# Late modulation vectors: from TensorE row products to VectorE dot products over transposed weights

## Chip, cores, metric

One core of a Trainium2 chip. The metric is device time in microseconds, the median of several executions. Engines: PE is TensorE, DVE is VectorE, ACT is ScalarE, POOL is GpSimd, SP is SyncE, which issues nearly all DMA here.

## The reference, cut to what matters

```python
mod = (silu(c) @ w_mod).reshape(1, 6, 1, -1)      # c: [1,1024], w_mod: [1024, 6*1024], bf16
sa, ca, ga, sb, cb, gb = mod[:, 0] ... mod[:, 5]  # six vectors of 1024
h = layernorm(x) * (1 + ca) + sa                  # x: [2048, 1024]
x = x + ga * attention(h)                         # 32 heads of 128, 512 keys, 4 kv heads
h = layernorm(x) * (1 + cb) + sb
x = x + gb * swiglu(h)                            # hidden size 3584
```

The vectors `sa` and `ca` are needed in the first microseconds. The other four are the late ones: `ga` at the end of the first attention chunk, `cb` and `sb` at the second norm, `gb` in the feed-forward part.

## The kernel before

The attention part runs in 128 steps (4 chunks of 512 rows, 32 heads). In each step PE does scores, a query projection, an output-projection unit and the product with v, and DVE evicts PSUM (copies PE's results out of its accumulator memory). `at(k, f, ...)` hangs a task on step k. The late vectors are made as rows: `silu(c)` is spread over 32 columns, and four narrow matmuls (128x32 weights) run side by side.

```python
sil32 = const.tile([P, DT, 32], BF16, name="sil32")
for dt in range(DT):                              # eight DVE broadcasts, in the start-up
    nc.vector.tensor_scalar(out=sil32[:, dt, :], in0=ones_bf[:, 0:32],
                            scalar1=siluc[:, dt:dt + 1], scalar2=None, op0=ALU.mult)
# ...
def mod_rows(n, part):                            # four calls: steps 5, 13, 21, 29
    ps = mm("row_ps")
    tiles = [wm_rows.pop(0) for _ in range(2)]
    for k in range(4):
        for i in range(4):                        # four column tiles: 16 matmuls a burst
            nc.tensor.matmul(ps[32 * i:32 * i + 32, :], lhsT=sil32[:, 4 * part + k, :],
                             rhs=tiles[i // 2][:, k, (i % 2) * 512:(i % 2 + 1) * 512],
                             start=(k == 0), stop=(k == 3))
    # ... evict, add the two parts, store rows to DRAM ...
def load_cols(n, k, dst, add_one):                # steps 16 and 32
    src = row_d[n][k:k + 2, :].rearrange("a (b p) -> p (a b)", p=P)
    fetch(out=dst, in_=src)                       # 1024 values come back as columns
    if add_one:                                   # only at step 16
        nc.vector.tensor_scalar(out=dst, in0=dst, scalar1=1.0, scalar2=None, op0=ALU.add)
```

The weight-norm bound (sums of squares of the weights, on DVE) already uses the instruction that the change will use, and four of its products are clipped to the same step 32:

```python
def bound_wq(hg, i, j):
    # ...
    pin(nc.vector.scalar_tensor_tensor(out=junk, in0=w, scalar=1.0, in1=w, op0=ALU.mult,
                                       op1=ALU.mult, accum_out=sq[:, col:col + 1]))
# ...
at((1 + hg % (NTC - 1)) * H + max(0, 4 * hg - 3 + 2 * i + j), bound_wq, hg, i, j)
```

The weight-norm bound (sums of squares of the weights, on DVE) already uses the instruction that the change will use.

The second norm: normalised rows (`xn`), crossbar transposes (the DMA transposes a block on its way), affine operations (times a vector, plus a vector).

Of the kernel before, what the change touches and what calls it, by code (L numbers as in the profile page):

```python
# [9 lines left out]
ALU = mybir.AluOpType  # L10
AX = mybir.AxisListType
BF16 = mybir.dt.bfloat16
FP32 = mybir.dt.float32
# [575 lines left out]
def fast_path(ctx, tc, flag, A_x, A_k_cache, A_v_cache, A_wq, A_wo, B_x, B_w_gate, B_w_up,  # L589
# [3 lines left out]
    nc = tc.nc  # L593
    P = 128
    _, S, D = A_x.shape
    _, Hkv, Sk, Dh = A_k_cache.shape
# [6 lines left out]
    TCW = 512  # L603
    NTC = S // TCW
    QT = TCW // P
    DT = D // P
# [17 lines left out]
    wm_v = w_mod.rearrange("(dt p) n -> p dt n", p=P)  # L624
# [4 lines left out]
    const = ctx.enter_context(tc.tile_pool(name="const", bufs=1))  # L629
    xpool = ctx.enter_context(tc.tile_pool(name="xres", bufs=1))  # L630
    hpool = ctx.enter_context(tc.tile_pool(name="hT", bufs=4))
# [3 lines left out]
    wk = ctx.enter_context(tc.tile_pool(name="work", bufs=2))  # L635
    sm = ctx.enter_context(tc.tile_pool(name="small", bufs=4))
    psp = ctx.enter_context(tc.tile_pool(name="psum", bufs=4, space=bass.MemoryType.PSUM))
    dp = ctx.enter_context(tc.tile_pool(name="dram", bufs=4, space=bass.MemoryType.DRAM))
# [7 lines left out]
    def blkC(name, shape, dt=BF16):  # L646
        return pc_.tile(shape, dt, name=name, tag="C")

    def mm(name, shape=(P, 512), dt=FP32):
        return psp.tile(list(shape), dt, name=name, tag="mm", bufs=4)  # L650
# [9 lines left out]
    def pin(ins, what="steps"):  # L660
        return tc.keep_in_program_order(ins) if stage[what] else ins

    def fetch(out, in_):
        pin(nc.sync.dma_start(out=out, in_=in_), "dma")  # L664

    def load(out, in_):
        with nc.allow_non_contiguous_dma(reason="weight slice"):
            fetch(out=out, in_=in_)
# [33 lines left out]
    for kv in range(Hkv):  # L702
        pin(nc.sync.dma_start_transpose(
            out=kT[:, kv, :], in_=A_k_cache[0, kv, k0:k0 + W, :]), "dma")
# [10 lines left out]
    ones_bf = const.tile([P, P], BF16, name="ones_bf")  # L715
# [15 lines left out]
    sa, ca1, sb, cb1 = (modT[:, i, :] for i in range(4))  # L731
    ga_bc = const.tile([P, D], FP32, name="ga_bc")
    gb_bc = const.tile([P, D], FP32, name="gb_bc")
# [7 lines left out]
    sil_r = const.tile([DT, P], BF16, name="sil_r")  # L741
# [3 lines left out]
    siluc = const.tile([P, DT], BF16, name="siluc")  # L745
# [12 lines left out]



    sil32 = const.tile([P, DT, 32], BF16, name="sil32")
    for dt in range(DT):
        nc.vector.tensor_scalar(out=sil32[:, dt, :], in0=ones_bf[:, 0:32],
                                scalar1=siluc[:, dt:dt + 1], scalar2=None, op0=ALU.mult)
    wm_rows = []
    row_part = []
    row_d = {}

    def load_rows(vec, part):
        t = hpool.tile([P, 4, D], BF16, name="wmr", tag="hT")  # L770
        load(t, wm_v[:, 4 * part:4 * part + 4, vec * D:(vec + 1) * D])
        wm_rows.append(t)

    def mod_rows(n, part):
        ps = mm("row_ps")
        tiles = [wm_rows.pop(0) for _ in range(2)]
        for k in range(4):
            for i in range(4):
                nc.tensor.matmul(ps[32 * i:32 * i + 32, :], lhsT=sil32[:, 4 * part + k, :],  # L779
                                 rhs=tiles[i // 2][:, k, (i % 2) * 512:(i % 2 + 1) * 512],  # L780
                                 start=(k == 0), stop=(k == 3))
        if part == 0:
            r = blkC("row", [P, TCW], FP32)
            nc.vector.tensor_copy(out=r, in_=ps)
            row_part.append(r)
        else:
            r = row_part.pop()
            nc.vector.tensor_tensor(out=r, in0=ps, in1=r, op=ALU.add)
            d = dp.tile([4, TCW], FP32, name="row_d", tag="row_d", bufs=2)
            fetch(out=d, in_=r[0:P:32, :])  # L790
            row_d[n] = d

    def load_gate(n, k, dst):
        fetch(out=dst.rearrange("p (a b) -> p a b", a=2),
                          in_=row_d[n][k:k + 2, :].partition_broadcast(P))

    def load_cols(n, k, dst, add_one):
        src = row_d[n][k:k + 2, :].rearrange("a (b p) -> p (a b)", p=P)
        with nc.allow_non_contiguous_dma(reason="1024 values to columns"):
            fetch(out=dst, in_=src)  # L800
        if add_one:
            nc.vector.tensor_scalar(out=dst, in0=dst, scalar1=1.0, scalar2=None, op0=ALU.add)

    tasks = {}

    def at(k, f, *a):
        tasks.setdefault(k, []).append((f, a))


    hT = {}  # L810
# [15 lines left out]
    def ln_norm(tt, on_act=False):  # L826
        mv = ln.pop(tt)
        n = wk.tile([P, D], BF16, name="xn", tag="xn", bufs=3)
        if on_act:
            nc.vector.scalar_tensor_tensor(out=mv[:, 3:4], in0=mv[:, 0:1], scalar=-1.0,  # L830
                                           in1=mv[:, 2:3], op0=ALU.mult, op1=ALU.mult)
            nc.scalar.activation(out=n, in_=xt[tt], func=ACT.Identity, bias=mv[:, 3:4],
                                 scale=mv[:, 2:3])
        else:
            pin(nc.vector.tensor_scalar(out=n, in0=xt[tt], scalar1=mv[:, 0:1],
                                        scalar2=mv[:, 2:3], op0=ALU.subtract, op1=ALU.mult))
        return n
# [85 lines left out]
    for t in range(QT):  # L923
        ln_stats(t)
        n = ln_norm(t, t % 2 == 0)
# [5 lines left out]
    for half in range(DH):  # L931
# [6 lines left out]
        for n in range(4 * LEAD):  # L938
            dt, g = (4 * half + n // LEAD, n % LEAD) if half == 0 else (4 + n % 4, n // 4)
            nc.tensor.matmul(q0_ps[g],  # L940
                             lhsT=wq_tiles[(0, 0, dt // 4)][:, dt % 4, g * P:(g + 1) * P],
                             rhs=hT[("h1", 0)][:, dt, :], start=(dt == 0), stop=(dt == DT - 1))
# [168 lines left out]
            nc.vector.tensor_tensor(out=x1, in0=f, in1=x1, op=ALU.add)  # L1111


    for n, vecs in enumerate(((2, 4), (5, 3))):
        for part in range(2):
            k = 16 * n + 8 * part
            at(k, load_rows, vecs[0], part)
            at(k + 2, load_rows, vecs[1], part)
            at(k + 5, mod_rows, n, part)
        at(16 * n + 15, load_gate, n, 0, gb_bc if n else ga_bc)  # L1120
        at(16 * n + 16, load_cols, n, 2, sb if n else cb1, n == 0)
    for tt in range(QT, S // P):
        cc, t = divmod(tt, QT)
        at(max((cc - 1) * H - 16, 0) + 2 + 2 * t, load_x, tt)
# [116 lines left out]
def kernel(tc, *args):  # L1241
    nc = tc.nc
    with tc.tile_pool(name="guard", bufs=1) as gp:
        flag = gp.tile([1, 1], I32, name="flag")
        fast_path(tc, flag, *args)
        over = nc.values_load(flag[0:1, 0:1], min_val=0, max_val=1)
        with tc.If(over > 0):
            general_path(tc, *args)
# [30 lines left out]
```

## Time and profile before

| | before |
|---|---|
| time, median of 3 | 1283.59 us (1283.0 to 1285.08) |
| PE busy | 1270.0 us, 99% of the span |
| DVE busy | 577.3 us, 45% |

The page of the kernel before: busy time by engine, and the chain of waits by engine.

```profile
PE 1270.0 (99%) x7601; PEld 643.1 (50%) x7601; DVE 577.3 (45%) x1271; ACT 333.9 (26%) x433; POOL 1.2 (0%) x8
...
PE 96%; DMA 2%; DVE 1%; SPq 0%; ACT 0%; issue 0%; DVEq 0%
```

PE is the bound. Only its work, or a stop of it, moves the time. The groups of instructions of the kernel before (busy us, mean ns of one, idle before with its releaser):

```profile
L955 DVE SCALAR_TENSOR_TENSOR junk<-wq 128x1024 bf16<-128x1024 bf16 x32 | 38.9, 1215 | 0.0
...
L779 PE MATMUL row_ps<-wmr,sil 128*32 128x512 bf16 x64 | 4.2, 382 | 0.0
...
L802 DVE TENSOR_SCALAR modT<-modT 128x8 f32<-128x8 f32 x1 | 0.2, 172 | 3.6 <-DMA modT<-row_d 3.6
```

The 64 row matmuls of 382 ns are busy for 4.2 us only, since four run at once. The add-one (L802) kept DVE idle for 3.6 us. The waits of the kernel before (us in total, times, longest):

```profile
DVE modT L802 <- DMA modT<-row_d: 3.6, 1, 3.6
...
PE mod_ps L753 <- DMA wm<-in_w_mod_dram: 1.7, 1, 1.7
...
PE a_ps L1096 <- DVE acc L1102: 1.0, 1, 1.0
...
PE gu_ps L1173 <- DVE guT L1179: 0.8, 1, 0.8
```

A row burst in the timeline of the kernel before (start us, duration us, engine, line, operation):

```profile
44.73 1.89 PE L1019 MATMUL q_ps<-hT,wq 128*128 128x512 bf16 x8
...
46.55 1.05 PE L779 MATMUL row_ps<-wmr,sil 128*32 128x512 bf16 x16
...
47.52 0.29 PE L1064 MATMUL o_ps<-v_sb,pT 128*128 128x130 bf16 x2
```

From the first row matmul to the next work is 0.97 us. The stop behind the add-one, same view:

```profile
86.93 0.43 SPq L664 DMA_DIRECT2D modT<-row_d  x1
...
92.00 0.17 DVE L802 TENSOR_SCALAR modT<-modT 128x8 f32<-128x8 f32 x1 [3.62 <-DMA modT<-row_d]
...
92.69 0.67 DVE L1102 COPY acc<-a_ps 128x512 f32<-128x512 f32 x1
...
93.41 1.89 PE L1096 MATMUL a_ps<-wo,oT 128*128 128x512 bf16 x8 [0.99 <-DVE acc L1102]
```

The column read was issued at 86.93 us. DVE stood until 92.00, the eviction behind it came late, and PE stood 0.99 us for a free PSUM bank.

The busiest stretch of DVE, by windows of 10 us (busy us and instructions of PE, PEld, DVE, ACT, POOL; clock; DMA share; GB/s):

```profile
210.00:220.00 10.00, 10.00 (x72) 5.53 (x70) 8.46 (x19) 3.84 (x7) 0.00 (x0) 1.00 0.53 121
220.00:230.00 10.00, 10.00 (x72) 5.53 (x70) 8.74 (x21) 3.84 (x6) 0.00 (x0) 1.00 0.66 196
230.00:240.00 10.00, 10.00 (x72) 5.54 (x70) 8.53 (x18) 3.43 (x5) 0.00 (x0) 1.00 0.84 241
240.00:250.00 10.00, 10.00 (x72) 5.52 (x70) 8.81 (x19) 3.75 (x4) 0.00 (x0) 1.00 0.16 36
```

### The profile page before, as it was taken

How to read it: one execution, taken by the hardware profiler on the slowest of the kernel's cores; microseconds unless marked ns; L12 is line 12 of the kernel's file. 1: busy time of each engine (PE TensorE's matmuls, PEld its weight loads, DVE VectorE, ACT ScalarE, POOL GpSimd, SP SyncE). 2: the span in 40 equal slices, each digit the busy share in tenths (PEclk: the TensorE clock that was granted, in tenths of full speed). 3: DMA queues.
4: the chain of work that ended last, by engine and by line, in shares of the span. 5: the costliest groups of instructions: out<-in, count | busy, mean ns of one | idle time of the engine just before them, and what ended most of it. 6: DMA issues, size and time to landing. Idle time of an engine off the chain costs nothing.

```text
span 1283.0 us, 18137 instructions
## 1 busy us (share of the span) xinstructions
PE 1270.0 (99%) x7601; PEld 643.1 (50%) x7601; DVE 577.3 (45%) x1271; ACT 333.9 (26%) x433; POOL 1.2 (0%) x8
## 2 busy tenths in 40 slices
PE   8999999999999999999999999999999999999998
PEld 4555555555555555555554444444444444444444
DVE  4464557865577755576663642221212221221122
ACT  3543334343333433333341111011100111011100
POOL 0000000000000000000000000000000000000000
PEclk8999999999999999999999999999999999999999
DMA  9878566557355554445678484454536455454401
GB/s 286 275 187 234 169 149 171 133 142 204 98 124 156 148 140 148 116 149 131 132 195 247 129 249 149 139 189 147 180 103 218 140 164 164 135 193 134 129 22 47
DMA packets 280108, 204.21 MB, mean 159 GB/s; under 512 B 113865, under 2 KB 273609, under 8 KB 280018
## 3 DMA queue, kind: packets, MB, share of 16 engines
q1 hardware_dynamic: 275106, 198.78, 54.1%
q10 hardware_dynamic: 4912, 4.20, 1.0%
q8 instruction: 61, 1.00, 0.3%
q14 instruction: 29, 0.24, 0.1%
HBM read 174.08 MB, written 4.21 MB: 139 GB/s over the span
## 4 chain that ended last, share of the span: by engine, by line
PE 96%; DMA 2%; DVE 1%; SPq 0%; ACT 0%; issue 0%; DVEq 0%
PE gu_ps L1173 29%; PE a_ps L1096 17%; PE q_ps L1019 17%; PE d_ps L1193 15%; PE o_ps L1064 9%; PE s_ps L1032 8%; DMA wm<-in_w_mod_dram 1%; DMA hT<-xn 1%; PE q_ps L940 0%; DMA modT<-row_d 0%; PE row_ps L779 0%; SPq L664 0%; PE mod_ps L753 0%; DVE st L816 0%; ACT pT L1034 0%; PE h_ps L927 0%
## 5 line engine op out<-in xcount | busy, mean ns | idle before, releaser
L1034 ACT ACTIVATE pT<-s_ps 128x1024 bf16<-128x1024 f32 x256 | 248.7, 1020 | 341.8 <-PE s_ps L1032 341.8
L1096 PE MATMUL a_ps<-wo,oT 128*128 128x512 bf16 x1024 | 241.9, 379 | 1.0 <-DVE acc L1102 1.0
L1019 PE MATMUL q_ps<-hT,wq 128*128 128x512 bf16 x1000 | 236.7, 379 | 0.3 <-DVE modT L755 0.3
L1173 PE MATMUL gu_ps<-hT,wg 128*128 128x512 bf16 x896 | 211.7, 379 | 0.8 <-DVE guT L1179 0.8
L1179 DVE TENSOR_TENSOR guT<-gu_ps,sg 128x512 bf16<-128x512 f32 x112 | 77.4, 691 | 282.5 <-ACT sg L1178 282.5
L1178 ACT ACTIVATE sg<-gu_ps 128x512 bf16<-128x512 f32 x112 | 66.9, 597 | 489.6 <-PE gu_ps L1173 438.4
L1193 PE MATMUL d_ps<-wd,guT 128*128 128x512 bf16 (+2 forms) x952 | 194.2, 366 | 0.0
L916 DVE CAST qT<-q_ps 128x512 bf16<-128x512 f32 x128 | 88.2, 691 | 176.9 <-PE q_ps L1019 176.3
L1173 PE MATMUL gu_ps<-hT,wu 128*128 128x512 bf16 x672 | 163.3, 379 | 0.0
L1096 PEld LDWEIGHTS <-oT 128*128 128x128 bf16 x1024 | 99.9, 98 | 122.3 <-issue 2.1
L1019 PEld LDWEIGHTS <-wq 128*128 128x128 bf16 x1000 | 97.8, 98 | 117.8 <-issue 0.3
L1193 PEld LDWEIGHTS <-guT 128*128 128x128 bf16 x952 | 90.9, 98 | 103.0
L1064 PEld LDWEIGHTS <-pT 128*128 128x128 bf16 x2048 | 126.6, 98 | 30.6 <-issue 0.4
L1173 PEld LDWEIGHTS <-wg 128*128 128x128 bf16 x896 | 87.6, 98 | 106.5 <-issue 1.1
L1064 PE MATMUL o_ps<-v_sb,pT 128*128 128x130 bf16 x2048 | 137.1, 220 | 0.0
L1032 PE MATMUL s_ps<-qT,kT 128*128 128x512 bf16 x512 | 131.5, 379 | 0.6 <-ACT pT L1034 0.6
L1173 PEld LDWEIGHTS <-wu 128*128 128x128 bf16 x672 | 65.8, 98 | 79.3
L1051 DVE TENSOR_TENSOR oq<-o_ps,rl 128x256 bf16<-128x256 f32 (+2 forms) x256 | 101.2, 419 | 4.3
L1197 DVE TENSOR_TENSOR f<-d_ps,gb_bc 128x512 f32<-128x512 f32 (+2 forms) x34 | 22.4, 660 | 147.1 <-PE d_ps L1193 147.1
L1104 DVE TENSOR_TENSOR acc<-a_ps,acc 128x512 f32<-128x512 f32 x64 | 44.0, 688 | 38.8 <-PE a_ps L1096 38.8
L1032 PEld LDWEIGHTS <-kT 128*128 128x128 bf16 x512 | 44.9, 98 | 31.7 <-issue 1.3
L1173 PE MATMUL gu_ps<-hT,v_sb 128*128 128x512 bf16 x224 | 57.5, 379 | 0.0
(77 smaller groups left out, 372.6 us busy)
## 6 DMA issues: line engine op xcount, KB each, us to landing
wq<-in_A_wq_dram SPq DMA_DIRECT2D x64, 512.0 KB, 4.2
wo<-in_A_wo_dram SPq DMA_DIRECT2D x64, 512.0 KB, 5.7
wg<-in_B_w_gate_dram SPq DMA_DIRECT2D x56, 512.0 KB, 4.5
wd<-in_B_w_down_dram SPq DMA_DIRECT2D x56, 512.0 KB, 7.1
wu<-in_B_w_up_dram SPq DMA_DIRECT2D x42, 512.0 KB, 5.9
wmr<-in_w_mod_dram SPq DMA_DIRECT2D x8, 1024.0 KB, 11.5
v_sb<-in_B_w_up_dram SPq DMA_DIRECT2D x14, 512.0 KB, 6.2
x<-in_A_x_dram SPq DMA_DIRECT2D x16, 256.0 KB, 5.7
```

Of the source, the lines that this page charges most:

```text
L916: nc.vector.tensor_copy(out=t, in_=q_ps)
L1019: nc.tensor.matmul(q_ps, lhsT=wq_tiles[(cc, h // 4, dt // 4)][:, dt % 4, (h % 4) * P:(h % 4 + 1) * P], rhs=hT[("h1", cc)][:, dt, :], start ...
L1032: nc.tensor.matmul(s_ps[:, i, :], lhsT=kT[:, kv, j * P:(j + 1) * P], rhs=qT[g], start=True, stop=True)
L1034: nc.scalar.activation(out=p[:, 2 * jj:2 * jj + 2, :], in_=s_ps, func=ACT.Exp, scale=scale)
L1051: nc.vector.tensor_tensor(out=dst, in0=ps[:, s0:s0 + cnt, 0:Dh], in1=sc, op=ALU.mult)
L1064: nc.tensor.matmul(o_slot["ps"][:, s_, :], lhsT=pT[g][:, j, t * P:(t + 1) * P], rhs=v_sb[:, kv, j, 0:VN], start=(j == 0), stop=(j == WT - 1))
L1096: nc.tensor.matmul(a_ps, lhsT=oT[(cc, 2 * q + i)][:, hh % 4, t * P:(t + 1) * P], rhs=wo_tiles[(cc, q, dh, i)][:, hh % 4, :], start=(hh == ...
L1104: nc.vector.tensor_tensor(out=acc[(cc, t)][:, dsl], in0=a_ps, in1=acc[(cc, t)][:, dsl], op=ALU.add)
L1173: nc.tensor.matmul(ps[:, n, :], lhsT=gu_w[(cc, fg, nm, dt // 4)][:, dt % 4, fi * P:(fi + 1) * P], rhs=hT[("h2", cc)][:, dt, :], start=(dt ...
L1178: nc.scalar.activation(out=g, in_=ps[:, 0, :], func=ACT.Silu)
L1179: nc.vector.tensor_tensor(out=guT[(cc, fg)][:, fi, :], in0=ps[:, 1, :], in1=g, op=ALU.mult)
L1193: nc.tensor.matmul(d_ps, lhsT=guT[(cc, f // 4)][:, f % 4, t * P:(t + 1) * P], rhs=wd_tiles[(cc, dh, f // 4)][:, f % 4, c0:c0 + w], start=( ...
```

## The change

The intent is to take the late vectors off PE. `silu(c)` is broadcast to all partitions. A block of 128 columns of w_mod is loaded transposed by the DMA crossbar, and one DVE instruction multiplies it by `silu(c)` and sums, giving 128 values as a column. `cb` and `sb` are then where they are needed. The gates `ga` and `gb`, which are needed as rows, leave through a 32x32 DVE transpose and DRAM. One transpose is issued every second step, and its dot product runs three steps later.

```diff
-    sil32 = const.tile([P, DT, 32], BF16, name="sil32")
-    ...                                    # eight broadcasts, load_rows, mod_rows, load_cols
+    def spread_c():
+        fetch(out=c_d, in_=sil_r)
+        fetch(out=c_bc.rearrange("p (a b) -> p a b", a=DT), in_=c_d.partition_broadcast(P))
+
+    def load_wmT(vec, j):
+        if j % 4 == 0:
+            wm_cols[(vec, j // 4)] = hpool.tile([P, 4, D], BF16, name="wmT", tag="hT")
+        c0 = vec * D + j * P
+        pin(nc.sync.dma_start_transpose(out=wm_cols[(vec, j // 4)][:, j % 4, :],
+                                        in_=w_mod[:, c0:c0 + P]), "dma")
+
+    def mod_dot(vec, j, dst):
+        t = wm_cols[(vec, j // 4)]
+        junk = wk.tile([P, D], BF16, name="junk", tag="junk", bufs=1)
+        pin(nc.vector.scalar_tensor_tensor(out=junk, in0=t[:, j % 4, :], scalar=1.0, in1=c_bc,
+                                           op0=ALU.mult, op1=ALU.mult,
+                                           accum_out=dst[:, j:j + 1]))
+    ...                                    # add_one, store_gate (nc.vector.transpose), load_gate
-    for n, vecs in enumerate(((2, 4), (5, 3))):
-        ...
+    at(0, spread_c)
+    for vec, dst, starts in ((2, gcol[0], (1, 9)), (4, cb1, (17, 25)), (3, sb, (33, 41)),
+                             (5, gcol[1], (51, 61))):
+        for part in range(2):
+            for i in range(4):
+                at(starts[part] + 2 * i, load_wmT, vec, 4 * part + i)
+                at(starts[part] + 2 * i + 3, mod_dot, vec, 4 * part + i, dst)
+        k = starts[1] + 10
+        if vec == 4:
+            at(k, add_one, cb1)
+        elif vec in (2, 5):
+            at(k, store_gate, vec // 5)
+            at(k + 3, load_gate, vec // 5, gb_bc if vec == 5 else ga_bc)
```

More of the change, by code (lines that the diff above doesn't have):

```diff
@@ L756, in mod_cols @@
                                 scalar1=1.0 if add_one else 0.0, scalar2=None, op0=ALU.add)
-    sil32 = const.tile([P, DT, 32], BF16, name="sil32")
-    for dt in range(DT):
-        nc.vector.tensor_scalar(out=sil32[:, dt, :], in0=ones_bf[:, 0:32],
-                                scalar1=siluc[:, dt:dt + 1], scalar2=None, op0=ALU.mult)
-    wm_rows = []
-    row_part = []
-    row_d = {}
-    def load_rows(vec, part):
-        t = hpool.tile([P, 4, D], BF16, name="wmr", tag="hT")
-        load(t, wm_v[:, 4 * part:4 * part + 4, vec * D:(vec + 1) * D])
-        wm_rows.append(t)
@@ L774, in mod_rows @@
-    def mod_rows(n, part):
-        ps = mm("row_ps")
-        tiles = [wm_rows.pop(0) for _ in range(2)]
-        for k in range(4):
-            for i in range(4):
-                nc.tensor.matmul(ps[32 * i:32 * i + 32, :], lhsT=sil32[:, 4 * part + k, :],
-                                 rhs=tiles[i // 2][:, k, (i % 2) * 512:(i % 2 + 1) * 512],
-                                 start=(k == 0), stop=(k == 3))
-        if part == 0:
-            r = blkC("row", [P, TCW], FP32)
-            nc.vector.tensor_copy(out=r, in_=ps)
-            row_part.append(r)
-        else:
-            r = row_part.pop()
-            nc.vector.tensor_tensor(out=r, in0=ps, in1=r, op=ALU.add)
-            d = dp.tile([4, TCW], FP32, name="row_d", tag="row_d", bufs=2)
-            fetch(out=d, in_=r[0:P:32, :])
-            row_d[n] = d
@@ L793, in load_gate @@
-    def load_gate(n, k, dst):
-        fetch(out=dst.rearrange("p (a b) -> p a b", a=2),
-                          in_=row_d[n][k:k + 2, :].partition_broadcast(P))
-    def load_cols(n, k, dst, add_one):
-        src = row_d[n][k:k + 2, :].rearrange("a (b p) -> p (a b)", p=P)
-        with nc.allow_non_contiguous_dma(reason="1024 values to columns"):
-            fetch(out=dst, in_=src)
-        if add_one:
-            nc.vector.tensor_scalar(out=dst, in0=dst, scalar1=1.0, scalar2=None, op0=ALU.add)
+    c_d = dp.tile([DT, P], BF16, name="c_d", tag="c_d", bufs=1)
@@ new lines, in fast_path @@
+    c_bc = const.tile([P, D], BF16, name="c_bc")
+    gcol = [const.tile([P, 32], FP32, name=f"gcol{n}") for n in range(2)]
+    grow = const.tile([P, 32], FP32, name="grow")
+    for n in range(2):
+        nc.gpsimd.memset(gcol[n], 0.0)
+    wm_cols = {}
+    col_d = {}
+    def spread_c():
[7 more added lines that the diff above has]
+                                        in_=w_mod[:, c0:c0 + P]), "dma")
@@ new lines, in mod_dot, with add_one, store_gate @@
+    def mod_dot(vec, j, dst):
[4 more added lines that the diff above has]
+                                           accum_out=dst[:, j:j + 1]))
+    def add_one(dst):
+        pin(nc.vector.tensor_scalar(out=dst, in0=dst, scalar1=1.0, scalar2=None, op0=ALU.add))
+    def store_gate(n):
+        d = dp.tile([DT, P], FP32, name="col_d", tag="col_d", bufs=2)
+        pin(nc.vector.transpose(out=grow, in_=gcol[n]))
+        for q in range(4):
+            fetch(out=d[:, 32 * q:32 * q + 32], in_=grow[32 * q:32 * q + DT, :])
+        col_d[n] = d
@@ L804, in fast_path, with load_gate @@
+    def load_gate(n, dst):
+        fetch(out=dst.rearrange("p (a b) -> p a b", a=DT), in_=col_d[n].partition_broadcast(P))
     tasks = {}
@@ L1111, in emit_wo @@
             nc.vector.tensor_tensor(out=x1, in0=f, in1=x1, op=ALU.add)
-    for n, vecs in enumerate(((2, 4), (5, 3))):
+    at(0, spread_c)
+    for vec, dst, starts in ((2, gcol[0], (1, 9)), (4, cb1, (17, 25)), (3, sb, (33, 41)),
+                             (5, gcol[1], (51, 61))):
         for part in range(2):
-            k = 16 * n + 8 * part
-            at(k, load_rows, vecs[0], part)
-            at(k + 2, load_rows, vecs[1], part)
-            at(k + 5, mod_rows, n, part)
-        at(16 * n + 15, load_gate, n, 0, gb_bc if n else ga_bc)
-        at(16 * n + 16, load_cols, n, 2, sb if n else cb1, n == 0)
+            for i in range(4):
[7 more added lines that the diff above has]
+            at(k + 3, load_gate, vec // 5, gb_bc if vec == 5 else ga_bc)
     for tt in range(QT, S // P):
```

## The prediction

> **What bounds the kernel now.** TensorE. The page's busy table gives PE 1270.0 of 1283.0 us (99%), VectorE (DVE) 577.3 (45%); the chain of waits is 96% PE, 2% DMA, 1% DVE. The granted clock is full in nearly all slices. Only PE time, or a PE wait, moves the total.
>
> **Removed.**
> - The 64 row matmuls (row_ps, 128x32 weights) that make the late vectors. Each shows 379 ns, but four column tiles run side by side: in the timeline a burst of 16 takes a PE slot of 0.98 us (46.54 to 47.52, 75.60 to 76.58). The Trainium skill, "TensorEngine Tiling (Array Packing)", Overview, states up to 4x for a dimension of at most 32; the trace agrees (64 matmuls, 4.2 us busy). Four bursts: 3.9 us, all critical.
> - A wait. The columns came back from DRAM and DVE's add-one sat idle 3.6 us for them (groups view, modT from DMA). There PE shows its only 1.0 us wait for DVE (a_ps on acc), and in 90 to 100 us PE is busy 9.01 of 10. Worth 1.0 us.
> - Eight DVE broadcasts of siluc (1.2 us) in the start-up, ahead of statistics that PE needs: 0 to 0.9 us.
>
> **Added.**
> - 32 DVE dot products. The weight-norm bound runs the same instruction on the same 128x1024 shape: 1215 ns plus 82 ns for the accumulator read. So 41 us more on DVE, over steps 4 to 70 (40 to 390 us), one per two steps of 5.2 us; DVE goes to about 617 us.
> - 32 crossbar transposes of 256 KB on the SP queue. Those of that size from SBUF (hT from xn) land in 3.2 us, those of k from DRAM (128 KB) in 5.2; issue takes 1.25 to 1.43. Their 256-byte packets take about 24 ns, so each costs about 1.5 us of the 16 engines (estimate), 48 us against 22 for the same bytes in 2 KB packets. "DMA: Bandwidth & Descriptors" puts the line-rate minimum at 512 bytes; here there is room (DMA share mostly 0.4 to 0.7 after 140 us). The dot comes three steps (10.5 to 15.6 us) after the issue.
> - Two gate round trips through DRAM, as before, with slack.
>
> **Where it can come back.** Between 210 and 250 us DVE is busy 8.5, 8.7, 8.5, 8.8 of each 10 us (last output projection, norm statistics and norm bound together). Four dots there make 34.5 + 4.9 = 39.4 of 40 us: it just fits. PE tolerates about 2.6 us of DVE delay (the 3.6 us stop cost 1.0), so I expect 0 to 2 us of PE waits, typically 0.5. Elsewhere DVE has 15 to 50% free.
>
> **Sum.** -3.9 (row matmuls) -1.0 (wait) -0.3 (start) +0.5 (crowded stretch) = -4.7: 1283.6 goes to 1279.0 us; range 1276.0 to 1283.5. Faster by over 2%: 1%; within: 97%; slower: 2%.
>
> **Right would show** no row_ps; PE busy down about 4 us; PE full at 90 to 100 us; DVE up about 37 us net; PE waits on DVE at 210 to 250 us below 2 us; dots of 1.2 us with hardly any idle before them. **Wrong would show** DVE idle ahead of dots on the transposes; PE waits on DVE of several us; transposes landing later than 10 us; a changed start-up.
>
> **What would make it wrong.** The first dot (about 40 us) needs the broadcast of c and a transpose issued while the queue is crowded (DMA share above 1.0 at 20 to 40 us); each late landing stops DVE, and PE beyond 2.6 us. The transposes read 256-byte rows 12 KB apart, which no transfer here does; their landing may be worse. Pinned dots may push evictions back.

## More of the kernel before

Step 32 and the late norm, timeline of the kernel before. In the first two lines the query matmuls of two steps start 5.23 us apart. The last two are the late norm, the last chunk's second norm, which runs inside the feed-forward part (four normalised rows, `xn`, in three buffers): its four transposes occupy the SP queue for 6.80 us, and PE then waits 0.83 us.

```profile
182.64 1.89 PE L1019 MATMUL q_ps<-hT,wq 128*128 128x512 bf16 x8
...
187.87 1.89 PE L1019 MATMUL q_ps<-hT,wq 128*128 128x512 bf16 x8
...
745.04 6.80 SPq L848 DMA_TRANSPOSE hT<-xn  x4
...
755.87 1.89 PE L1173 MATMUL gu_ps<-hT,wg 128*128 128x512 bf16 x8 [0.83 <-DVE guT L1179]
```

## The result, and the profile after

| | before | after |
|---|---|---|
| time, median of 6 runs each | 1284.17 us (1283.0 to 1285.14) | 1277.19 us (1276.31 to 1278.34) |
| ratio | | 0.9946, 95% interval 0.9933 to 0.9958 |
| DVE busy | 577.3 us | 606.8 us |

A ratio is the mean time of one kernel's runs over that of the other's runs of the same rounds, so it is not quite the ratio of the medians. The kernel became 7.0 us faster (difference of the medians), where 4.7 was forecast.

The page of the changed kernel, busy time and chain:

```profile
PE 1256.8 (99%) x7396; PEld 641.0 (50%) x7537; DVE 606.8 (48%) x1325; ACT 333.7 (26%) x433; POOL 1.3 (0%) x10
...
PE 97%; DVE 1%; issue 1%; ACT 0%; DMA 0%
```

PE's busy time is not to be read here: PE has 7396 matmul records against 7537 weight loads, so 141 matmul records are missing, and the 13.2 us fall is partly that. The marks below do not suffer from it. The dots, in the groups of the changed kernel:

```profile
L786 DVE SCALAR_TENSOR_TENSOR junk<-wmT,c_bc 128x1024 bf16<-128x1024 bf16 x32 | 38.9, 1216 | 0.0
```

They last what the norm bound's product lasted, and DVE never stood idle before one: the transposes were always in time. The place of the first burst, in the timeline of the changed kernel:

```profile
43.79 1.89 PE L1018 MATMUL q_ps<-hT,wq 128*128 128x512 bf16 x8
...
45.52 1.07 PE L1063 MATMUL o_ps<-v_sb,pT 128*128 128x130 bf16 x16
```

From query matmuls to next work is 1.73 us now against 2.79 before. The crowded stretch, windows of the changed kernel, moved by the 6 us that it runs earlier:

```profile
204.00:214.00 10.00, 9.95 (x71) 5.52 (x71) 9.42 (x21) 3.70 (x7) 0.00 (x0) 1.00 0.59 145
214.00:224.00 10.00, 9.95 (x71) 5.52 (x71) 9.02 (x22) 3.70 (x6) 0.00 (x0) 1.00 0.71 210
224.00:234.00 10.00, 9.89 (x70) 5.52 (x71) 10.00 (x21) 3.43 (x5) 0.00 (x0) 1.00 0.76 193
234.00:244.00 10.00, 9.95 (x70) 5.52 (x70) 9.84 (x21) 3.64 (x4) 0.00 (x0) 1.00 0.54 140
```

DVE is nearly full (38.3 of 40 us, where the prediction computed 39.4), but no PE wait falls here (the missing hundredths of PE are missing records). Step 32, timeline of the changed kernel:

```profile
173.54 1.22 DVE L786 SCALAR_TENSOR_TENSOR junk<-wmT,c_bc 128x1024 bf16<-128x1024 bf16 x1
...
175.29 1.22 DVE L954 SCALAR_TENSOR_TENSOR junk<-wq 128x1024 bf16<-128x1024 bf16 x1
...
176.23 1.89 PE L1018 MATMUL q_ps<-hT,wq 128*128 128x512 bf16 x8
...
176.55 1.22 DVE L954 SCALAR_TENSOR_TENSOR junk<-wq 128x1024 bf16<-128x1024 bf16 x1
...
177.90 1.22 DVE L954 SCALAR_TENSOR_TENSOR junk<-wq 128x1024 bf16<-128x1024 bf16 x1
...
179.38 1.22 DVE L954 SCALAR_TENSOR_TENSOR junk<-wq 128x1024 bf16<-128x1024 bf16 x1
...
181.76 1.89 PE L1018 MATMUL q_ps<-hT,wq 128*128 128x512 bf16 x8
```

A dot and four norm-bound products fall into one step, and the query matmuls now start 5.53 us apart, against 5.23 before. The late norm, timeline of the changed kernel:

```profile
738.94 5.29 SPq L847 DMA_TRANSPOSE hT<-xn  x4
...
742.27 0.55 DVE L834 TENSOR_SCALAR xn<-x,mvl 128x1024 bf16<-128x1024 bf16 x1 [1.84 <-DMA hT<-xn]
...
748.77 1.89 PE L1177 MATMUL gu_ps<-hT,wg 128*128 128x512 bf16 x8
```

The transposes take 5.29 us instead of 6.80, and PE doesn't wait. The change doesn't touch this place.

**Marks.** The steady part repeats to some hundredths of a microsecond, so two traces can be set against each other step by step. The mark of a step is the start of its first score exponential on ACT. The table gives each trace's marks minus those of the first trace of before; "late norm" is an operation just behind it (the 18th gating product). Bursts of before lie ahead of the marks 6, 14, 22 and 30, the add-one ahead of 17, the four norm-bound products between 33 and 36.

```
trace            step 4    6     14     17     22     30     36    124   late norm
before (again)    +0.38  +0.39  +0.39  +0.16  +0.16  +0.16  +0.16  +0.16  -0.13
after             -0.93  -2.02  -3.10  -4.25  -5.33  -6.41  -6.10  -6.10  -7.10
after (again)     -1.07  -2.15  -3.23  -4.38  -5.47  -6.55  -6.25  -6.25  -7.24
```

In the first trace after, the start gives -0.93, four bursts give -1.08 each (sum -4.33 before rounding), the add-one's wait -1.15, step 32 takes back 0.31, nothing happens from step 36 to 124 (the crowded stretch included), and the late norm gives -1.00. The experiments test each term.

### The profile page after: what moved, and what is told of

Read it like the earlier page. It is cut to its first block, busy times and chain, and to the rows that moved or that the text cites. A ratio compares the mean times of both kernels' runs of the same rounds, so it can differ in the third digit from the quotient of the medians. Undisturbed runs are those within 1.5% of the kernel's fastest.

```text
span 1275.8 us, 17958 instructions
## 1 busy us (share of the span) xinstructions
PE 1256.8 (99%) x7396; PEld 641.0 (50%) x7537; DVE 606.8 (48%) x1325; ACT 333.7 (26%) x433; POOL 1.3 (0%) x10
## 3 DMA queue, kind: packets, MB, share of 16 engines
q1 hardware_dynamic: 302866, 199.03, 54.6%
## 4 chain that ended last, share of the span: by engine, by line
PE 97%; DVE 1%; issue 1%; ACT 0%; DMA 0%
PE gu_ps L1177 30%; PE a_ps L1095 17%; PE q_ps L1018 17%; PE d_ps L1197 15%; PE o_ps L1063 9%; PE s_ps L1031 8%; PE q_ps L939 1%; DVE junk L954 0%; DVE st L815 0%; DMA x<-in_A_x_dram 0%; PE mod_ps L753 0%; ACT pT L1033 0%; DVE qT L915 0%; ACT xn L831 0%; PE h_ps L926 0%
```

## The experiments

My theory: the gain is PE time of the bursts plus the add-one's wait, less a DVE crowding at step 32. Rivals: the DMA pattern (8 MB of w_mod in early 1 MB loads before, spread out after), or chance in the start-up and at the late norm. Each kernel ran five times beside the kernel before, and all gave correct results.

### before_again and after_again: what repeats

No edit.

> The unchanged kernel before, once more, to see which marks of the trace repeat. Theory: within 0.3 us of itself up to the late norm (first score exponential at 28.3 us, step 20 at 112.3 us, step 124 at 657.7 us in the first trace); the 0.9 us PE wait at the late norm (755 us) is chance of the DMA and may be absent: ratio 1.000, all runs within 1283 to 1285.2. Rival: the 0.9 us wait is a fixed part of the kernel before and stands here too.

> The changed kernel, once more. Theory: ratio 0.9946 +- 0.0008 (1276.3 to 1278.3 us), the same marks: -0.93 us at the first exponential, -4.25 at step 20, -6.10 from step 36 to the end of attention, and anything from -6.1 to -7.1 at the end, as the late norm falls. Rival: the change always removes the late-norm wait, so -7.1 at the end.

Measured: before_again 1284.06 us, ratio 0.9994 (0.998 to 1.0007); after_again 1277.33, ratio 0.9943 (0.993 to 0.9957). The marks are in the table above: bursts and step 32 repeat to 0.01 us. At the start before_again was 0.38 us off, a little more than the 0.3 expected. The add-one's wait was 0.23 us shorter in before_again, so it was worth about 0.9 to 1.15. The late norm is 0.29 us shorter in before_again, not by the 1.0 us of both traces of the changed kernel. So the wait is not constant, and pure chance is not enough to explain it either.

### before_latesil and after_sil8: is the start-up gain the eight broadcasts?

```diff
 before_latesil: the eight broadcasts become a task
-    for dt in range(DT): nc.vector.tensor_scalar(out=sil32[:, dt, :], ...)
+    at(0, spread_sil)
 after_sil8: the same eight, dead, at their old place in the changed kernel
```

> The kernel before with its eight broadcasts of the silu vector moved out of the start-up to step 0. The order of TensorE's start-up then equals that of the changed kernel. Theory that the start-up gain is these broadcasts: first exponential 0.9 us earlier (27.4 us), everything after it shifted alike, 1282.6 to 1283.5 us (-0.9). Rival that the start-up gain is DMA timing or that the w_mod loads matter: under 0.3 us.

> The changed kernel with the eight dead broadcasts put back at the place they had, so that the start-up of TensorE has the order of the kernel before. Theory that the start-up order earns something through where the half-clock stretch falls: a half-clock stretch at 12.5 to 14.4 us as in the kernel before (the changed order has it at 21 to 24 us, or not at all), first exponential at 26.9 to 28.7 us, timed runs 0.5 to 1.3 us above those of the changed kernel (1277.2), ratio 0.9950 to 0.9955. Rival that the start-up is chance alone: half-clock stretch anywhere, ratio 0.9943 to 0.9946. The rest of the trace as in the changed kernel: -5.2 from the first exponential to step 124, late norm -1.0.

Measured: before_latesil 1284.74 us, ratio 1.0003 (0.999 to 1.0017); after_sil8 1277.53, ratio 0.9947 (0.9933 to 0.9961).

The theory fell. Taking the broadcasts out of the start-up put the first exponential at 28.84 us (before: 28.32 and 28.71), no earlier. Putting them in put it at 25.99 (after: 27.39 and 27.25), no later. They do move something: PE's program order in the start-up changes, and the half-clock stretch (a time in which the profile lists PE's granted clock at one half) begins at 12.5 to 14.4 us in the traces with the old order but at 21 to 24 us, or not at all, in those with the new one (an exception: before_pad64 has the old order and had it at 22.5). after_sil8 had it at 13.2, as expected, and was none the worse.

In the traces of changed kernels the start goes with this clock. The stretch is 3.41 or 6.83 us long, or absent. With none, the four traces of changed kernels reach the first exponential at 25.65 to 26.09 us; with 3.4 us at 21 us, at 27.39 and 27.25; with 6.8 us there, at 29.75 (a trace that also has the slow packets told of below). One exception is after_sil8, whose 3.4 us at 13.2 us cost nothing that shows (25.99). The clock is not all: with the same 3.4 us at 22.5 and 23.6 us, before_pad64 and before_latesil come at 28.63 and 28.84. The Trainium skill, "TensorE: Matmul & The Clock Gate", Part 1, describes a half-rate state and a free-running window of about 3.4 us; the lengths in these traces agree.

### before_lateadd: the add-one's wait

```diff
-        if add_one:                          # at step 16
-            nc.vector.tensor_scalar(out=dst, in0=dst, scalar1=1.0, ...)
+    at(22, add_one, cb1)
```

> The kernel before with only the add-one on the returned columns moved from step 16 to step 22, when the columns have long landed. Theory: the 3.6 us idle time of VectorE and TensorE's 1.0 us wait go; steps from 18 on are 1.1 us earlier, total -1.1 us (1282.4 to 1283.5), no other mark moves. Rival: the wait is caused by the row matmuls or by crowded DMA and reappears elsewhere: under 0.3 us.

Measured: 1283.31 us, ratio 0.9989 (0.9975 to 1.0002). In the marks the step from 14 to 17 is -1.15 us (from -0.97 to -2.12), exactly as in the changed kernel, and no other mark of the attention moves. DVE idled 0.0 us before the add-one. This part of the gain needs no dot products, only a wait placed later.

### after_rows4 and after_rows16: what a burst costs

```diff
+    def dead_rows(...):                      # narrow matmuls as before, of resident x; no reader
 after_rows4:  at(5, 13, 21, 29)  16 matmuls each
 after_rows16: at(2, 4, ... 32)    4 matmuls each
```

> The changed kernel with the 64 row matmuls put back as dead work, four bursts of 16 at steps 5, 13, 21 and 29, without an eviction or a load of w_mod rows. Theory that the gain of the steady part is TensorE time: each burst costs 1.08 us (0.86 us of matmuls, four abreast at 216 ns, and 0.22 us of switching to the narrow tiles and back), +4.3 us in all: ratio to before about 0.998. Rival that the gain came from the smaller early DMA crowding or from VectorE: under 1 us.

> The changed kernel with the same 64 matmuls as dead work, in sixteen bursts of four. Theory that a burst costs a switch of about 0.22 us besides 0.216 us for each four matmuls: 16 x 0.43 = +6.9 us, ratio to before about 1.000. Rival that only the matmuls cost: +3.5 to 4.3 us, as with four bursts.

Measured: after_rows4 1280.8 us, ratio 0.9967 (0.9954 to 0.9981); after_rows16 1283.43, ratio 0.9992 (0.9978 to 1.0006).

```
trace            step 4    6     14     17     22     30     36    124   late norm
after_rows4       -1.89  -1.89  -1.89  -3.04  -3.04  -3.04  -2.74  -2.74  -3.73
after_rows16      -1.67  -2.32  -1.66  -1.94  -2.15  -1.49  -0.40  -0.40  -0.52
```

With four dead bursts every step of -1.08 us is gone, and the wait of step 17 and the 0.31 at step 32 stay. From step 4 to 124 the changed kernel gains 5.17 us and this one 0.85: 4.32 us for four bursts. No w_mod rows were loaded, so the DMA pattern has no part in this term. The ratio is a little below the expected 0.998; this trace had a fast start (step 4 at -1.89).

With sixteen bursts of four the part from step 4 on costs 6.44 us for the 15 bursts that lie in it, 0.43 each. Solving the two (16 matmuls 1.08, four 0.43) gives about 0.217 us for each four matmuls and 0.21 us for each burst, at both sizes. The first agrees with the spacing of full-width matmuls ((1890 - 379) / 7 = 216 ns in a group of eight above). "TensorEngine Tiling (Array Packing)", Key Properties, says that a change of tiling mode drains the engine; these runs show a fixed 0.21 us for going narrow and back, which fits, though they don't show what it consists of. One such burst, in the timeline of after_rows16:

```profile
41.38 0.40 PE L779 MATMUL row_ps<-x,ones_bf 128*32 128x512 bf16 x4
```

### after_spread: the 0.31 us at step 32

```diff
-        at((1 + hg % (NTC - 1)) * H + max(0, 4 * hg - 3 + 2 * i + j), bound_wq, hg, i, j)
+        at((1 + hg % (NTC - 1)) * H + 4 * hg - 3 + 2 * i + j, bound_wq, hg, i, j)
```

> The changed kernel with the four norm-bound products that share step 32 spread over steps 29 to 32. Theory that the 0.31 us given back between steps 32 and 36 is that burst of four with a dot on top: the mark of step 36 is 0.3 us earlier (-6.4 against before), total -0.3 us. Rival that it is the dots' transposes or another wait: no change.

Measured: 1276.38 us, ratio 0.9937 (0.9923 to 0.995). The marks go from -7.55 at step 30 to -7.56 at step 36, where the changed kernel lost 0.31. The burst with a dot on top is the cause. 0.3 us is below what the timed ratios tell apart.

### after_dots2: how much room DVE has

```diff
-        pin(nc.vector.scalar_tensor_tensor(..., accum_out=dst[:, j:j + 1]))
+        for out_d in (dot2, dst):
+            pin(nc.vector.scalar_tensor_tensor(..., accum_out=out_d[:, j:j + 1]))
```

> The changed kernel with every dot product done twice (41 us more on VectorE). Theory that the dots are free only because VectorE just has room: in the stretch of steps 37 to 44 (200 to 245 us) VectorE is past full and TensorE waits there, +2 to +5 us over that stretch, +0.5 to 1.5 us at step 32, nothing elsewhere; total +3 to +6 us. Rival that VectorE has slack anywhere and the queue of four PSUM banks hides it: under 1 us in all.

Measured: 1280.86 us, ratio 0.9964 (0.9951 to 0.9978). In the marks, step 32 costs 1.06 us instead of 0.31, the stretch of steps 43 to 52 costs 0.70, all else almost nothing: about 1.5 us more than the changed kernel in the steady part. The timed difference is larger; in the one trace the rest is a slow start (the first exponential came at 29.75 us), which the edit doesn't explain. Windows of after_dots2:

```profile
217.00:227.00 10.00, 9.95 (x71) 5.44 (x70) 10.00 (x23) 3.90 (x7) 0.00 (x0) 1.00 0.85 223
227.00:237.00 10.00, 9.74 (x68) 5.27 (x68) 10.00 (x21) 4.11 (x5) 0.00 (x0) 1.00 0.81 170
237.00:247.00 10.00, 9.89 (x67) 5.34 (x67) 10.00 (x22) 3.21 (x4) 0.00 (x0) 1.00 0.60 159
247.00:257.00 10.00, 9.83 (x64) 5.12 (x63) 10.00 (x25) 4.26 (x6) 0.00 (x0) 1.00 0.52 86
```

DVE is full for 40 us on end, and PE pays only 0.70 us. The places were right, and the size that I expected (2 to 5 us for the stretch) was too large: a backlog on DVE is carried on and worked off later.

### before_pad64 and before_xn4: the late norm

The DMA packets of the trace show a thing that the edits share. Instructions come in packets of 16 KB, which the profile counts with the data on the core's 16 DMA engines, 61 or 62 in a run, about 1 us each. In the traces of before one of them starts 1.9 us ahead of the first late transpose. In those of the changed kernel the nearest is 13 us away. The change removes 128 PE instructions. The 61 packets of before bring its 15202 matmuls and weight loads, about 250 each, so that is half a packet. This agrees with the 16 KB for 256 instructions that the Trainium skill, "Runtime: NRT & Kernel Launch", Instruction fetch mechanics, states; the page calls the cost mostly hidden.

```diff
 before_pad64:
+    at(7, pad_pe)                # 64 dead one-column matmuls: 128 more PE instructions
 before_xn4:
-        n = wk.tile([P, D], BF16, name="xn", tag="xn", bufs=3)
+        n = wk.tile([P, D], BF16, name="xn", tag="xn", bufs=4)
```

> The kernel before with 64 dead one-column matmuls (128 TensorE instructions, half of a 16 KB instruction packet) added at step 7. Theory that the late-norm gain is where an instruction fetch falls: the instruction packet that now starts 1.9 us before the first late transpose moves some 13 us away, the fourth row normalisation comes under 4.1 us after the first transpose instead of 4.7 to 5.5, and the mark after the late norm moves by -0.5 to -1.0 us against the end of attention (before: -0.3 to +0.4), while the 64 matmuls cost 2 to 4 us at step 7. Rival that the late wait belongs to something else of the kernel before: it stays as it was (fourth normalisation at 4.7 to 5.5 us).

> The kernel before with four buffers instead of three for the normalised rows. Theory that the late norm's length comes from the fourth row waiting for the first transpose to land: the fourth normalisation follows the first at once (under 1 us after the first transpose), the last affine ends earlier, and the 0.8 us TensorE wait there shrinks or goes although the instruction packet still falls 1.9 us ahead: mark after the late norm -0.6 to -1.0 against the end of attention. Rival that the transposes' own landing decides: wait unchanged within 0.3 us.

Measured: before_pad64 1286.64 us, ratio 1.0012 (0.9998 to 1.0026); before_xn4 1284.46, ratio 0.9998 (0.9984 to 1.0011).

```
trace            step 4    6     14     17     22     30     36    124   late norm
before_pad64      +0.31  +0.31  +1.91  +4.60  +4.60  +4.60  +4.60  +4.60  +3.61
before_xn4        -0.43  -0.43  -0.43  -0.54  -0.54  -0.54  -0.54  -0.54  -0.29
```

In before_pad64 the packet lies 13.6 us after the first late transpose, the fourth normalised row follows that transpose by 3.75 us (before: 4.99), and the late norm gains 0.99 us, as in the changed kernel, without any part of the change. Its matmuls cost 1.60 us (2 to 4 were expected); the 2.69 us ahead of mark 17 are a longer add-one wait (PE waited 2.0 us there) and a second half-clock stretch of 3.4 us at 97.6 us. The late transposes of before_pad64 on the SP queue:

```profile
749.65 5.56 SPq L854 DMA_TRANSPOSE hT<-xn  x4
```

In before_xn4 the fourth row waited for nothing (0.8 us after the first transpose) and the late norm gained nothing (+0.24). So the wait for a third buffer is not the cause; what is left is the course of the transposes themselves.

All traces together (change from step 124 to behind the late norm, against the first trace of before): with a packet just ahead, before 0.00 and -0.29, before_latesil -0.24, before_lateadd +0.43, before_xn4 +0.24, after_rows16 -0.12, after_rows4 -0.99; without one, after -1.00 and -1.00, after_dots2 -0.83, after_spread -0.99, after_spread_xn4 -1.00, before_pad64 -0.99, after_sil8 -0.56. Two do not fit: after_rows4 had the packet and lost nothing, and after_sil8 had none and its fourth row still came at 4.76 us. before_pad64, one trace, says that the place of the packet matters; it is not the whole cause. One sign sorts all fourteen: the time that the SP queue took to issue the second of the four transposes. It was 1.26 to 1.60 us wherever the late norm gained 0.8 to 1.0, and 2.17 to 2.38 wherever it did not (after_sil8, which gained 0.56: 2.19). What holds that issue up in after_sil8, without a packet near, stays open.

### after_spread_xn4: the version suggested by the rest

```diff
 after_spread, and:
+        n = c_bc if tt == S // P - 1 else wk.tile([P, D], BF16, name="xn", tag="xn", bufs=3)
```

> The changed kernel with the norm-bound products spread over steps 29 to 32 and the last normalised row in its own buffer (the broadcast of c, dead by then). Theory: -0.31 us at step 32 as before, late-norm mark at its best, -1.0 whatever the fetch does; ratio 0.993 to 0.994, 1276 to 1277 us. Rival: something new waits: 0.995 or more.

Measured: 1277.15 us, ratio 0.994 (0.9926 to 0.9953). The marks show no loss at step 32 (-7.47 at 30 and 36) and -1.00 at the late norm, as after_spread has them already. Timed, it can't be told from the changed kernel or from after_spread. I would keep the spreading alone.

## Why the prediction was right, point by point

The time, 1277.19 us, lies in the range, and the direction and main mechanism held. The centre, 1279.0, was short by about 2 us, the size of two gains that the prediction did not have, about 1.4 us at the start and 0.7 at the late norm; that the time still fell inside owes something to a range 7.5 us wide. Term by term:

- **Row matmuls, "-3.9".** Right in mechanism, mis-sized: 4.33 us. I read the slot from the first row matmul to the next work. The narrow mode costs also ahead of its first matmul; from a full-width matmul to the next, the burst was 1.08 us, of which 0.21 is switching (after_rows4, after_rows16).
- **The wait, "-1.0".** Right: 1.15 us against the first trace, 0.9 against the second, and before_lateadd shows the cause.
- **Start, "-0.3".** The step that failed: the broadcasts ahead of the statistics earn nothing that is shown (before_latesil, after_sil8). The changed kernel did start faster, by 0.93 us in its trace. In the timed runs of before and after_again the means differ by 7.12 us, of which the marks of after_again against before_again account for 4.96 between steps 4 and 124 and 0.71 at the late norm, which leaves about 1.4 for the start (an estimate from these numbers). Two things go with it. First, in the first 22 us the 1 KB DMA packets took on average 50.0 to 50.6 ns in all six traces of before and its variants and in after_dots2, the slowest starter of all, and 46.2 to 47.0 in the other seven. Second, the same split stands in PE's waits: for the first loads of w_mod (mod_ps from DMA wm, L753) PE waited 1.4 to 2.7 us in the first seven, 1.9 on average, and 0 to 1.0 in the others, 0.5 on average (the first trace of after waited 0.7 us for DVE there instead). The gain most likely falls at this wait, and the size fits, but no edit has shown it, and what makes the packets slower stays open. after_dots2 differs from the changed kernel only from 45 us on, so no edit that I can name sets it.
- **Crowded stretch, "+0.5".** The size was near (0.31), the place wrong. At 210 to 250 us DVE just fitted, about as computed, and PE lost nothing. The loss came where four norm-bound products are clipped to step 32, which windows of 10 us had averaged away: DVE was busy 8.31 of 10 us there, and no burst could be seen. after_spread shows it.
- **Not foreseen:** the late norm's 0.7 to 1.0 us, which padding alone gives as well (before_pad64). It goes with where things fall in a program of this length and not with the idea; how much of it is the instruction packet stays open.
- **"DVE up about 37 us".** It rose 29.5. Instructions on DVE overlap by about 0.08 us (in the timeline the operation behind a dot of 1.22 us starts 1.14 or 1.15 us after it), so busy time of packed instructions is less than the sum of their durations. Summed, the durations rose by 37.8 us (630.2 to 668.0), as forecast.
- **Transposes, "48 us against 22".** They were in time, and no dot waited. The main DMA queue's packets took 54.6% of the span instead of 54.1%, about 2.5 us more of 16 engines (0.546 x 1275.8 - 0.541 x 1283.0), although packets under 512 bytes went from 113865 to 145601. The extra cost didn't show, partly because the 256-byte packets took 21 ns on average instead of the 24 assumed, partly because the other packets were quicker.

## What to carry to other kernels

When one engine is busy 99% of the time, moving 4 us of its work to an engine with room gained those 4 us here, and the new work cost only where the other engine's queue was already full for several operations on end; look for that in single steps, not in windows. Compare two traces by marks of one repeating operation: differences of 0.1 us become readable in a run whose start-up alone varies by 2 us and more. Before crediting a gain far from the edit, check whether an unrelated padding of the program gives it too.

## What the Trainium skill lacked or had wrong

- "TensorEngine Tiling (Array Packing)" states that a mode switch drains, without a size: a fixed 0.21 us for each visit to the 128x32 mode (after_rows4, after_rows16), so bursts should be few and long.
- "Runtime: NRT & Kernel Launch" calls the crossing of a 16 KB instruction block mostly hidden. It does not speak of what a fetch may do to other transfers. Here a fetched packet took about 1 us; with one 1.9 us ahead of four transposes, PE lost up to 1.0 us, and a padding of half a block gave it back (before_pad64, one trace). after_rows4 and after_sil8 show that this is not the whole story.
- "VectorE: DVE Perf Modes", The three transpose paths, gives 1309 ns for a 128x128 crossbar transpose, without saying from what to what that runs. Here the SP queue was held 1221 ns (median of 32) to issue one eight times as large, 1024x128 from DRAM rows 12 KB apart; its landing is not in the trace, but no dot three steps later waited for it.
- "DMA: Bandwidth & Descriptors" puts the line-rate minimum at 512 bytes. Nothing was wrong there, only a size is added: median 18 ns for a 256-byte packet and 46 ns for one of 1 KB, so 14 against 22 bytes/ns; it cost this kernel nothing.
- No page that I drew on tells why the same start-up loads run at 50 ns per 1 KB packet in some programs and 46.5 in others, nor that this goes with 1.4 us more of PE waiting.
